# Seven partial products in layer one's second and third pair, and the x sums of that layer made in its first pair

## The chip, the core and the metric

One core of a Trainium2 chip runs the whole program: the attention, then two feed-forward layers. Its engines are TensorE (PE; its weight loads are listed as PEld), VectorE (DVE), ScalarE (ACT), GpSimd (POOL) and SyncE (SP), which issues the transfers. Each engine takes its own instructions in order; between engines, semaphores hold an instruction until what it needs is there. The metric is the device time of one execution in microseconds (us).

## What is computed

```python
def _attn_ref(q, k, v, centroids):          # clustered attention, 2 x 8 heads, 768 x 64
    ...
    return np.matmul(attn, v)

def _moe_ref(x, w_in, w_out):               # layer one; x is 1536 x 512, d_ff 2048
    h = x @ w_in
    g = np.maximum(0.01 * h, h)
    return g @ w_out

def _moe2_ref(x, w_in, w_out):              # layer two, the same sizes
    h = x @ w_in
    r = np.maximum(h, 0.0)
    return (r * r) @ w_out
```

## The kernel before

Every float32 operand of a matmul is split into a high and a low part (`xh`, `xl` for x; `wh`, `wl` for a weight block; `gh`, `gl` for an activation), and each product of two operands is three matmuls: high by high, low by high, high by low.

The attention fills `xh` and `xl` one pair of heads at a time. For the last pair, `xsplit` writes both parts on POOL (L275 the high part, L627 the low part, from the tile `xt`).

A feed-forward layer works through d_ff in eight pairs of blocks of 128 (f = 0, 2, .., 14), and x stands in three blocks of 512 rows. A step of the first kind ("plain") is `g1` (L950: one block of h from 4 x 3 matmuls of 128x512), `acts` (L960: ACT makes `gh` at L976 and the activated h at L977, DVE the low part `gl` at L982) and `g2` (L993: four output tiles of 3 matmuls each). In the first pair the results of `g2` are copied to `acc` by ACT (L1027), in later pairs added by DVE (L1030). `acc`, `th` and `tl` lie in memory that the attention has used, so the first writes to them wait for the last readers of it.

For row blocks 0 and 1 a pair can be worked out with seven products of half the inner size in place of eight (`seven`, L1054). On the way into the layer these are P1 to P7, each 2 x 3 matmuls; they need sums of weight blocks (`sum_pieces`, L246: four POOL instructions at L267, then the split, ACT L186 and POOL L187) and sums of x, called t1 to t4, made once for each of two inner blocks kk = 0 and 1 by `t_ops` (L1267). For these, DVE first adds high and low part back together (`whole`: w12, w11, w22, w21, at L1277), POOL forms t1 to t4 (L1283), ACT writes the high parts (`th`, L1286), POOL the low parts (`tl`, L1289). t4 is written over one of the x blocks, last of all (`t_last`: ACT L1326, DVE L1327). Between the products ACT and DVE carry intermediate results (`keep` L1075: k1, k6, k5; `add` L1063: aV, aX, aW); aX reads the tile that P4 then goes on adding to, so P4 waits for it. On the way out of a pair there are M1 to M7 (L1170), with one more block of weight sums.

Before, layer one runs as follows: pairs f = 0 and f = 2 are plain throughout; f = 4 is plain on the way in (steps g00, g01, g10, g11) and has seven products on the way out; from f = 6 on there are seven on both ways. Block 2 of the rows is always plain. The x sums are spread over the steps of f = 0 and 2 by the table `SUMS`; the weight blocks arrive and are taken apart by the table `TURN` (a pair of numbers is a block and a piece of its work: 0 the load, 1 ACT's and POOL's first pass, 2 DVE's join at L225, 3 ACT's high part, 4 POOL's low part). The landing buffer `wraw` is single: a block's transfer starts when the join of the block before has ended.

The order of instructions on PE, DVE, ACT and POOL is that of the program text from f = 2 on (`manual_schedule`). In pair f = 0 a scheduler places them.

Of the kernel before, what the change touches and what calls it, by code (L numbers as in the profile page):

```python
# [99 lines left out]
def attention_moe_moe_kernel(  # L100
# [1230 lines left out]
    def step_list(m, f, prev):  # L1331
# [68 lines left out]

    def sums(m, turn):
        for op in SUMS[m].get(turn, "").split():
            name, kk = op.split(".")
            t_by[m][int(kk)][name]()

    prev = []
    for m in range(2):
        turn = 0
        for f in range(0, NF, 2):
            if (m, f) == (0, 2):  # L1410
                order.enter_context(
                    tc.manual_schedule(
                        engines={
                            mybir.EngineType.PE,
                            mybir.EngineType.DVE,
                            mybir.EngineType.Activation,
                            mybir.EngineType.Pool,
                        }
                    )
                )  # L1420
# [7 lines left out]
            for i, step in enumerate(seq):  # L1428
                step()
# [11 lines left out]
                if (m, f + 2) == SEVEN[0] and i == 8:  # L1441
                    piece((*after, 3), 0)
                sums(m, turn)
                turn += 1

# [46 lines left out]
```

## Time and profile before

| | us |
|---|---|
| median of 3 runs | 737.61 (737.54 to 737.67) |
| profiled execution, its own time | 737.28 |
| span from the first to the last instruction of it | 735.6 |
| around the span | 1.7 |
| PE busy | 729.3 (99%) |
| POOL busy | 580.0 (79%) |
| DVE busy | 555.2 (75%) |
| ACT busy | 491.3 (67%) |

The attention runs to about 250 us of the span, layer one from 231 (the two overlap) to about 480, layer two to the end. Starts of instructions are counted from the span's start. A matmul's shown length is longer than the distance to the next one, since matmuls are pipelined; distances are read from starts. A DVE, ACT or POOL instruction that is listed as running may in part be held up inside; its length then exceeds that of its kind elsewhere.

### The profile page before, as it was taken

To read this page: it belongs to the slowest core of one execution; us is meant where nothing else is said; L and a number is where in the kernel's file an instruction comes from. 1 tells how busy PE (TensorE), PEld (TensorE's weight loads), DVE (VectorE), ACT (ScalarE), POOL (GpSimd) and SP (SyncE) were. 2 spreads that over 40 slices of the span, in tenths; PEclk is the share of its full clock that TensorE was granted. 3 is DMA by queue.
4 is the path that set the end of the run, shared out by engine and by line. 5 is a ranking of instruction groups with operands and counts; after the bars stand their busy time and mean duration, and the time that the engine had idled before them with its cause. 6 is when DMAs were issued, how large, how long until landed. Compare 5 with 4: busy or idle time off the path is not lost.

```text
span 735.6 us, 11900 instructions
## 1 busy us (share of the span) xinstructions
PE 729.3 (99%) x4264; PEld 647.3 (88%) x4264; DVE 555.2 (75%) x879; ACT 491.3 (67%) x909; POOL 580.0 (79%) x534
## 2 busy tenths in 40 slices
PE   9999999999999999999999999999999999999998
PEld 8999999999998888888888888888888898888987
DVE  7999999999998535476766867787676685866847
ACT  7988988988998464456364473657748457484561
POOL 7999999999957648766787877899798786777841
PEclk9999999999999999999999999999999999999999
DMA  5694574572602311111131121211113112121004
GB/s 150 168 224 111 108 186 111 113 180 68 160 22 95 121 70 60 57 58 57 59 115 57 58 91 54 85 57 58 58 58 115 57 58 61 60 110 57 1 1 172
DMA packets 17755, 65.57 MB, mean 89 GB/s; under 512 B 3120, under 2 KB 6320, under 8 KB 12704
## 3 DMA queue, kind: packets, MB, share of 16 engines
q1 hardware_dynamic: 17696, 64.81, 30.0%
q8 instruction: 34, 0.56, 0.3%
q14 instruction: 25, 0.20, 0.1%
HBM read 43.02 MB, written 3.15 MB: 63 GB/s over the span
## 4 chain that ended last, share of the span: by engine, by line
PE 94%; ACT 2%; DVE 2%; POOL 1%; issue 1%; POOLq 0%; ACTq 0%; DVEq 0%
PE h L933 33%; PE o L1170 17%; PE h L1170 10%; PE A L597 8%; PE S L500 8%; PE T L562 7%; PE o L1011 7%; PE S L370 1%; ACT e L532 1%; DVE nm L522 1%; PE warm L310 1%; DVE el L579 1%; ACT eh L573 0%; PE dots L370 0%; POOL e L549 0%
## 5 line engine op out<-in xcount | busy, mean ns | idle before, releaser
L933 PE MATMUL h<-xl,wh 128*128 128x512 f32 x288 | 112.3, 390 | 0.0
L933 PE MATMUL h<-xh,wl 128*128 128x512 f32 x288 | 112.2, 390 | 0.0
L933 PE MATMUL h<-xh,wh 128*128 128x512 f32 x288 | 112.2, 391 | 0.0
L1124 POOL TENSOR_TENSOR gl<-t,gh 128x512 fp32r<-128x512 f32 x52 | 73.1, 1426 | 36.4 <-ACT gh L1121 26.5
L579 DVE TENSOR_TENSOR el<-T,eh 128x512 fp32r<-128x512 f32 x144 | 94.6, 683 | 2.9 <-ACT eh L573 2.2
L549 POOL TENSOR_SCALAR e<-e,r 128x768 f32<-128x768 f32 x96 | 86.3, 908 | 12.7 <-PE T L562 6.8
L532 ACT ACTIVATE e<-S,nm 128x768 f32<-128x768 f32 x96 | 87.3, 909 | 9.8 <-DVE ds L398 5.3
L522 DVE TENSOR_REDUCE nm<-S 128x1 f32<-128x768 f32 x96 | 90.9, 948 | 3.6 <-PE S L370 1.9
L187 POOL TENSOR_TENSOR wl<-ws,wh 128x1024 fp32r<-128x1024 f32 x25 | 60.5, 2419 | 41.8 <-ACT wh L186 41.8
L500 PE MATMUL S<-hb 128*128 128x384 f32 (+1 forms) x384 | 89.5, 347 | 0.1
L187 POOL TENSOR_TENSOR wl<-wt,wh 128x1024 fp32r<-128x1024 f32 x31 | 76.0, 2451 | 12.9 <-ACT wh L186 12.2
L573 ACT CAST eh<-T 128x512 fp32r<-128x512 f32 x144 | 79.7, 590 | 8.8 <-PE T L562 8.6
L597 PE MATMUL A<-eh,vv 128*128 128x256 f32 x288 | 80.3, 308 | 0.6 <-DVE xt L619 0.6
L562 PE MATMUL T<-ident,e 128*128 128x128 f32 x576 | 79.7, 273 | 0.5 <-POOL e L549 0.5
L597 PE MATMUL A<-el,vv 128*128 128x256 f32 x288 | 73.0, 283 | 0.2 <-DVE el L579 0.2
L562 PEld LDWEIGHTS T<-ident,e 128*128 128x128 f32 x576 | 68.9, 143 | 3.6 <-POOL e L549 0.7
L212 ACT ACTIVATE wt<-wraw 128x1024 f32<-128x1024 f32 (+1 forms) x33 | 36.7, 1111 | 49.6 <-POOL ws L267 46.3
L1063 DVE TENSOR_TENSOR h<-h,q 128x512 f32<-128x512 f32 x36 | 25.2, 699 | 54.2 <-PE h L933 48.6
L933 PEld LDWEIGHTS h<-xh,wh 128*128 128x128 f32 x288 | 54.1, 188 | 12.0 <-DVE gl L1124 0.9
L933 PEld LDWEIGHTS h<-xh,wl 128*128 128x128 f32 x288 | 54.0, 188 | 11.3
L500 PEld LDWEIGHTS S<-hb 128*128 128x128 f32 (+1 forms) x384 | 62.2, 189 | 1.6 <-ACT e L532 1.4
L933 PEld LDWEIGHTS h<-xl,wh 128*128 128x128 f32 x288 | 54.1, 188 | 10.6
(190 smaller groups left out, 2051.0 us busy)
## 6 DMA issues: line engine op xcount, KB each, us to landing
wraw<-w SPq DMA_DIRECT2D x32, 1024.0 KB, 4.7
hb<-spl SPq DMA_DIRECT2D x14, 576.0 KB, 4.7
hb<-spl SPq DMA_DIRECT2D x42, 192.0 KB, 5.1
rqk<-qk SPq DMA_DIRECT2D x16, 384.0 KB, 3.7
rv<-v SPq DMA_DIRECT2D x8, 384.0 KB, 3.3
out<-q SPq DMA_DIRECT2D x11, 256.0 KB, 2.2
hb<-st SPq DMA_DIRECT2D x56, 24.0 KB, 1.9
hb<-hb SPq DMA_DIRECT2D x5, 144.0 KB, 8.1
```

Of the source, the lines that this page charges most:

```text
L187: return lambda eng=nc.gpsimd: eng.tensor_tensor(out=wl, in0=t, in1=wh.bitcast(F32), op=ALU.subtract)
L500: nc.tensor.matmul(out=s[:, c, 0:HALF], lhsT=hb[0:k, a, i * 128 : (i + 1) * 128], rhs=hb[0:k, b, c * HALF : (c + 1) * HALF], start=(a == 0 ...
L522: nc.vector.tensor_reduce(out=n, in_=s_t[t][:, :, 0:HALF], axis=AX.XY, op=ALU.max, negate=True)
L532: nc.scalar.activation(out=e.rearrange("p (a b) -> p a b", a=2), in_=s_t.pop(t)[:, :, 0:HALF], func=AF.Exp, bias=n_t.pop(t), scale=1.0, ac ...
L549: nc.gpsimd.tensor_scalar(out=e_t[t], in0=e_t[t], scalar1=r_t[t // 2][:, t % 2 : t % 2 + 1], scalar2=1.0, op0=ALU.mult, op1=ALU.mult,)
L562: nc.tensor.transpose(T[:, o : o + 128], e_t[2 * u + b][:, kc * 128 : (kc + 1) * 128], ident)
L573: nc.scalar.copy(out=eh[:, 2 * g : 2 * g + 2, :].rearrange("p a b -> p (a b)"), in_=T_t[u, g])
L579: nc.vector.tensor_tensor(out=el[:, 2 * g : 2 * g + 2, :].rearrange("p a b -> p (a b)"), in0=T_t.pop((u, g)), in1=eh[:, 2 * g : 2 * g + 2, ...
L597: nc.tensor.matmul(out=A, lhsT=w, rhs=m[:, kc, :], start=(kc == 0 and i == 0), stop=(kc == KC - 1 and i == 1),)
L933: nc.tensor.matmul(out=out, lhsT=l, rhs=r, start=(first and i == 0), stop=(i == n - 1), skip_group_check=not first,)
L1124: eng.tensor_tensor(out=lo[n], in0=full[n], in1=hi[n].bitcast(F32), op=ALU.subtract)
L1170: nc.tensor.matmul(out=out, lhsT=l, rhs=r, start=(fresh and i == 0), stop=(stop and i == 2), skip_group_check=True,)
```

## The change

Pair f = 2 of layer one gets seven products on both ways, pair f = 4 on the way in as well. The table `SEVEN_TOP` orders f = 2; f = 4 uses the table that f = 6 and later use. The x sums of both inner blocks are all made in pair f = 0; of the second inner block t1, t2 and t3, and of both blocks the low parts of t1 and t2, are made by DVE. The program's order is kept from step 7 of f = 0 on, not from f = 2 on. Block 2's hidden tiles lie in other PSUM banks.

```diff
-SEVEN_PLAIN = (
...
+SEVEN_TOP = (
+    "c3.0 P1 k1 P2 aV B11h B11f bh0 P6 k6 P5 k5 B11l c3.1 c3.2 h4.0 h4.1 n0.1 bh1 P7 aX B22h B22f P3 aW n0.2 "
...
-    PLAIN = (3, 1)
+    PLAIN = (1, 1)
...
-    SEVEN = tuple((0, f) for f in range(4, NF, 2)) + tuple((1, f) for f in range(2, NF, 2))
+    SEVEN = tuple((0, f) for f in range(2, NF, 2)) + tuple((1, f) for f in range(2, NF, 2))
...
-        for name, n, b, block in (
-            ("g00", "V", 0, f0), ("g01", "U", 0, f1), ("g10", "W", 1, f0), ("g11", "X", 1, f1)
-        ):
...
-            st[f"u{j}"] = bank(1 + j * m)
+            st[f"u{j}"] = bank(1 + j * (m or f == 2))
...
-            (0, 4): SEVEN_PLAIN, (0, NF - 2): SEVEN_LAST, (1, 2): SEVEN_SEAM, (1, NF - 2): SEVEN_END
+            (0, 2): SEVEN_TOP, (0, NF - 2): SEVEN_LAST, (1, 2): SEVEN_SEAM, (1, NF - 2): SEVEN_END
...
-        def minus(out, x, y, *tag):
+        def minus(out, x, y, *tag, eng=nc.gpsimd):
             st[out] = tmp(*tag)
-            nc.gpsimd.tensor_tensor(out=st[out], in0=st[x], in1=st[y], op=ALU.subtract)
+            eng.tensor_tensor(out=st[out], in0=st[x], in1=st[y], op=ALU.subtract)
...
+            "t1D": lambda: minus("t1", "b12", "b11", eng=nc.vector),
+            "t2D": lambda: minus("t2", "b22", "t1", eng=nc.vector),
+            "t3D": lambda: minus("t3", "b22", "b12", eng=nc.vector),
+            "l1D": lambda: low(0, "t1", nc.vector),
+            "l2D": lambda: low(1, "t2", nc.vector),
...
-            7: "w12.0 w11.0", 8: "t1.0 w22.0", 9: "t2.0", 10: "h1.0",
...
+            3: "w12.0 w11.0 t1.0", 4: "w22.0 t2.0 t3.0 w21.0", 5: "t4.0 w12.1",
+            7: "h1.0 h2.0 l1D.0 l2D.0 n2.0 w11.1 t1D.1 w22.1 t2D.1 h3.0 h1.1 l0.0",
+            8: "l3.0 t3D.1 w21.1 h2.1 n2.1 t4.1 n2.2 l1D.1 l2D.1", 9: "h3.1 l3.1",
...
-            if (m, f) == (0, 2):
-                order.enter_context(
...
+                if (m, i) == (0, 7):
+                    order.enter_context(
```

What this makes of the order of instructions stands at three places. The numbers behind the names tell tiles apart; line numbers of the changed program are two higher in the attention and four lower in `t_ops`.

POOL in the first pair, from its first pass over the weight block `wraw_3849` to the low part of x of the last heads (`xl`, from `xt_3518`). Before:

```order
L219 TENSOR_SCALAR wraw_3849<-wraw_3849 128x1024
L1283 TENSOR_TENSOR q_3971<-q_3949,q_3951 128x512
L275 TENSOR_SCALAR xh_66<-xt_3518 128x768
L1283 TENSOR_TENSOR q_3991<-q_3973,q_3971 128x512
L627 TENSOR_TENSOR xl_67<-xt_3518,xh_66 128x768
```

Now:

```order
L221 TENSOR_SCALAR wraw_3849<-wraw_3849 128x1024
L1279 TENSOR_TENSOR q_3874<-q_3870,q_3872 128x512
L277 TENSOR_SCALAR xh_66<-xt_3518 128x768
L1279 TENSOR_TENSOR q_3900<-q_3898,q_3874 128x512
L1279 TENSOR_TENSOR q_3902<-q_3898,q_3870 128x512
L269 TENSOR_TENSOR ws_3971<-wt_3895 128x256
L629 TENSOR_TENSOR xl_67<-xt_3518,xh_66 128x768
L189 TENSOR_TENSOR wl_3946<-wt_3895,wh_3945 128x1024
L1279 TENSOR_TENSOR t4_3923<-q_3904,q_3900 128x512
```

One more x sum (t3 of kk = 0) and the first of the four weight sums stand ahead of the low part of x; t4 of kk = 0 stands behind the weight block that follows it.

DVE in the first pair, from the join of the same weight block (`wt_3889`, now `wt_3895`) to the low part `gl_3845` of the first activated tile of row block 1. Before:

```order
L225 SCALAR_TENSOR_TENSOR wt_3889<-wt_3889,wraw_3849 128x1024
L982 TENSOR_TENSOR gl_3845<-h_3831,gh_3844 128x512
L982 TENSOR_TENSOR gl_3884<-h_3870,gh_3883 128x512
L982 TENSOR_TENSOR gl_3923<-h_3909,gh_3922 128x512
L982 TENSOR_TENSOR gl_3967<-h_3953,gh_3966 128x512
```

Now:

```order
L227 SCALAR_TENSOR_TENSOR wt_3895<-wt_3895,wraw_3849 128x1024
L1273 TENSOR_TENSOR q_3904<-xh_66,xl_67 128x512
L1273 TENSOR_TENSOR q_3925<-xh_66,xl_67 128x512
L1285 TENSOR_TENSOR tl_3777<-q_3874,th_3776 128x512
L1285 TENSOR_TENSOR tl_3777<-q_3900,th_3776 128x512
L1273 TENSOR_TENSOR q_3976<-xh_66,xl_67 128x512
L1279 TENSOR_TENSOR q_3978<-q_3925,q_3976 128x512
L984 TENSOR_TENSOR gl_3845<-h_3831,gh_3844 128x512
L1273 TENSOR_TENSOR q_3980<-xh_66,xl_67 128x512
L984 TENSOR_TENSOR gl_3890<-h_3876,gh_3889 128x512
```

Six instructions of the x sums stand between the join and `gl_3845` where none stood. The two that write `tl` wait for ACT's `th`. On ACT, too, three casts to `th` (q_3874, q_3900, q_3902) now stand between the four copies to `acc` and the activation `gh_3844`, which before followed the copies at once.

PE at the end of the first pair's row block 0, from the first matmul that reads the last heads' high part of x for `h_3831`. Before:

```order
L933 MATMUL h_3831<-xh_66,wh_3589 128x512
L933 MATMUL h_3870<-xh_66,wh_3803 128x512
L933 MATMUL h_3909<-xh_66,wh_3589 128x512
L933 MATMUL h_3953<-xh_66,wh_3803 128x512
L933 MATMUL h_3831<-xl_67,wh_3589 128x512
```

Now:

```order
L935 MATMUL h_3831<-xh_66,wh_3589 128x512
L935 MATMUL h_3876<-xh_66,wh_3803 128x512
L935 MATMUL h_3927<-xh_66,wh_3589 128x512
L935 MATMUL h_3831<-xl_67,wh_3589 128x512
L935 MATMUL h_3831<-xh_66,wl_3590 128x512
L935 MATMUL h_3876<-xl_67,wh_3803 128x512
L935 MATMUL h_3876<-xh_66,wl_3804 128x512
L935 MATMUL h_3927<-xl_67,wh_3589 128x512
L935 MATMUL h_3927<-xh_66,wl_3590 128x512
L1013 MATMUL o_3951<-gh_3844,wh_3589 128x512
L1013 MATMUL o_3951<-gl_3845,wh_3589 128x512
L1013 MATMUL o_3951<-gh_3844,wl_3590 128x512
```

The fourth hidden tile's twelve matmuls (`h_3953`, now `h_3988`) no longer stand in front of the reads of `xl` and `gl_3845` but behind the first half of the outputs `o_3951` to `o_3963`. Counted in the order, the first matmul that reads `xl` stood 32 matmuls ahead of the first matmul of pair f = 2 and now stands 42 ahead; the first that reads `gl_3845` stood 20 ahead and now stands 35 ahead. The number of instructions on PE in front of pair f = 2 is the same in both programs.

## Rows read from the trace of the kernel before

**Rows 1.** The page: busy us (share) and instructions by engine.

```profile
PE 729.3 (99%) x4264; PEld 647.3 (88%) x4264; DVE 555.2 (75%) x879; ACT 491.3 (67%) x909; POOL 580.0 (79%) x534
```

**Rows 2.** Waits of PE: waiter <- releaser: us in total, times, longest us.

```profile
PE warm L310 <- POOL ident masks.py:199: 1.4, 1, 1.4
PE A L597 <- DVE xt L619: 0.6, 1, 0.6
```

**Rows 3.** Timeline of PE: start us, length us, instruction, [idle before <- releaser].

```profile
258.18 0.39 PE L933 MATMUL h<-xl,wh 128*128 128x512 f32 x1
...
265.51 0.39 PE L933 MATMUL h<-xh,wh 128*128 128x512 f32 x1
...
334.87 0.39 PE L933 MATMUL h<-xh,wh 128*128 128x512 f32 x1
```

**Rows 4.** Timeline of POOL, up to the low part of the last heads' x.

```profile
248.03 1.12 POOL L219 TENSOR_SCALAR wraw<-wraw 128x1024 int32<-128x1024 uint32 x1 [1.28 <-DMA wraw<-w]
250.44 1.29 POOL L1283 TENSOR_TENSOR q<-q 128x512 f32<-128x512 f32 x1 [1.29 <-DVE q L1277]
251.70 1.27 POOL L275 TENSOR_SCALAR xh<-xt 128x768 fp32r<-128x768 f32 x1
252.95 2.25 POOL L1283 TENSOR_TENSOR q<-q 128x512 f32<-128x512 f32 x1
255.16 1.84 POOL L627 TENSOR_TENSOR xl<-xt,xh 128x768 fp32r<-128x768 f32 x1
```

**Rows 5.** Timeline of DVE, around x sums, a join and a `gl`.

```profile
249.61 0.68 DVE L1277 TENSOR_TENSOR q<-xh,xl 128x512 f32<-128x512 f32 x1
...
250.82 1.46 DVE L1277 TENSOR_TENSOR q<-xh,xl 128x512 f32<-128x512 f32 x1
252.21 1.84 DVE L225 SCALAR_TENSOR_TENSOR wt<-wt,wraw 128x1024 int32<-128x1024 int32 x1
...
270.66 1.23 DVE L225 SCALAR_TENSOR_TENSOR wt<-wt,wraw 128x1024 int32<-128x1024 int32 x1 [0.42 <-ACT wt L212]
271.81 1.77 DVE L1277 TENSOR_TENSOR q<-xh,xl 128x512 f32<-128x512 f32 x1
...
285.93 0.69 DVE L982 TENSOR_TENSOR gl<-h,gh 128x512 fp32r<-128x512 f32 x1 [0.33 <-ACT h L977]
```

**Rows 6.** Timeline of POOL, beside and after those, and a 128x768 scaling alone.

```profile
229.44 0.90 POOL L549 TENSOR_SCALAR e<-e,r 128x768 f32<-128x768 f32 x1
...
256.96 2.40 POOL L187 TENSOR_TENSOR wl<-wt,wh 128x1024 fp32r<-128x1024 f32 x1
...
271.16 1.87 POOL L1289 TENSOR_TENSOR tl<-q,th 128x512 fp32r<-128x512 f32 x1 [10.61 <-ACT th L1286]
...
285.68 1.30 POOL L1283 TENSOR_TENSOR q<-q 128x512 f32<-128x512 f32 x1 [1.23 <-DVE q L1277]
...
291.00 0.75 POOL L267 TENSOR_TENSOR ws<-wt 128x256 f32<-128x256 f32 x1
```

**Rows 7.** Timeline of ACT: the first copies to `acc`, an activation, a weight split.

```profile
254.08 1.05 ACT L186 CAST wh<-wt 128x1024 fp32r<-128x1024 f32 x1 [2.58 <-DVE wt L225]
257.04 2.06 ACT L1027 COPY acc<-o 128x512 f32<-128x512 f32 x4 [1.90 <-POOL xl L627]
258.95 0.64 ACT L976 ACTIVATE gh<-h 128x512 fp32r<-128x512 f32 x1
...
268.43 0.60 ACT L976 ACTIVATE gh<-h 128x512 fp32r<-128x512 f32 x1 [2.02 <-PE h L933]
```

**Rows 8.** Timeline of PE at the very start: its first matmuls, then six more.

```profile
1.41 4.21 PE L310 MATMUL warm<-ident 128*128 128x128 f32 x18 [1.41 <-POOL ident masks.py:199]
...
5.62 1.05 PE L310 MATMUL warm<-ident 128*128 128x128 f32 x6
```

**Rows 9.** Windows of the whole core: each engine's busy us (instructions), clock, DMA.

```profile
360.00:400.00 40.00, 40.00 (x178) 33.01 (x177) 27.95 (x42) 19.35 (x29) 31.02 (x25) 1.00 0.20 69
```

**Rows 10.** The page's transfers: out <- in, queue, kind xcount, KB each, us to landing.

```profile
wraw<-w SPq DMA_DIRECT2D x32, 1024.0 KB, 4.7
```

More of the change, by code (lines that the diff above doesn't have):

```diff
@@ L77 @@
 )
-SEVEN_PLAIN = (
-    "n0.1 g00 B11h B11f c3.1 c3.2 bh0 n0.2 B11l n1.0 g01 B21h B21f B21l bh1 n0.3 n0.4 g10 B12f T1 n1.1 "
-    "n1.2 g11 B22h B22f T3 T2 T1h T2h T1l T4 u0 T2l u0h u0f u0l T3h T3l n1.3 n1.4 "
-) + SEVEN_REST + " h4.0 h4.1"
+SEVEN_TOP = (
[4 rows of a table added]
+)
 SEVEN_TWO = SEVEN_FIRST.replace("B11h B11f P5 k5", "B11h P5 k5 B11f").replace(
@@ L1089, in seven @@
             )
-        for name, n, b, block in (
-            ("g00", "V", 0, f0), ("g01", "U", 0, f1), ("g10", "W", 1, f0), ("g11", "X", 1, f1)
-        ):
-            ops[name] = lambda n=n, b=b, block=block: prod(
-                n, [w_in(block, k) for k in ks], [x_in(k, b) for k in ks], True
-            )
         for name, n in (("k1", "U"), ("k6", "U"), ("k5", "W")):
@@ L1279, in whole, with low @@
             )
-        def minus(out, x, y, *tag):
+        def minus(out, x, y, *tag, eng=nc.gpsimd):
             st[out] = tmp(*tag)
-            nc.gpsimd.tensor_tensor(out=st[out], in0=st[x], in1=st[y], op=ALU.subtract)
+            eng.tensor_tensor(out=st[out], in0=st[x], in1=st[y], op=ALU.subtract)
         def high(i, t):
             nc.scalar.copy(out=th[:, i, kk], in_=st[t])
-        def low(i, t):
-            nc.gpsimd.tensor_tensor(
+        def low(i, t, eng=nc.gpsimd):
+            eng.tensor_tensor(
                 out=tl[:, i, kk], in0=st[t], in1=th[:, i, kk].bitcast(F32), op=ALU.subtract
@@ L1365, in attention_moe_moe_kernel @@
     TURN = (
-        ((0, 1),), ((0, 2),), ((1, 0),), ((0, 3),), ((0, 4), (1, 1)),
-        ((1, 2),), ((2, 0),), ((1, 3), (1, 4), (3, 0)), ((2, 1),), ((2, 2),),
+        ((0, 1),), ((0, 2),), ((1, 0),), ((0, 3),), ((0, 4), (1, 1)), ((1, 2),), ((1, 3), (1, 4)),
     )
@@ L1399, in attention_moe_moe_kernel, with sums @@
     t_by = [[t_ops(m, kk) for kk in range(2)] for m in range(2)]
-    def sums(m, turn):
+    def sums(m, turn, after, later):
         for op in SUMS[m].get(turn, "").split():
             name, kk = op.split(".")
-            t_by[m][int(kk)][name]()
+            if name in t_by[m][0]:
+                t_by[m][int(kk)][name]()
+            else:
+                piece((*(after if name[0] == "n" else later), int(name[1])), int(kk))
     prev = []
     for m in range(2):
-        turn = 0
         for f in range(0, NF, 2):
-            if (m, f) == (0, 2):
-                order.enter_context(
[L1412 to L1420, printed above, removed]
             after = pair_after(m, f)
@@ L1428, in attention_moe_moe_kernel @@
             for i, step in enumerate(seq):
+                if (m, i) == (0, 7):
+                    order.enter_context(
+                        tc.manual_schedule(
+                            engines={
+                                mybir.EngineType.PE,
+                                mybir.EngineType.DVE,
+                                mybir.EngineType.Activation,
+                                mybir.EngineType.Pool,
+                            }
+                        )
+                    )
                 step()
@@ L1440, in attention_moe_moe_kernel @@
                     piece((*later, k - 3) if k > 2 else (*after, k), j, *eng)
[L1441 to L1444, printed above, removed]
+                sums(m, i, after, later)
 _OUT = (1536, 512)
```

6 rows, old and new, of tables (SEVEN_TOP, SUMS) are left out of this document.

## The prediction

> **What bounds the kernel now.** I read the page's busy line first, then PE's waits, then the engines' timelines at the two places that the change reorders. PE is busy for 729.3 of 735.6 us [rows 1], which alone proves little, since matmuls overlap. The waits settle it: after the start, PE's longest wait is 0.6 us [rows 2]. The pace is even as well: from the first matmul of pair f = 2 at 265.51 to that of f = 6 at 334.87 [rows 3] there are 306 matmuls in the order, all of 512 columns: 69.36 / 306 = 0.2267 us each. So a matmul less is worth 0.2267 us, as long as PE goes on finding its operands; and any wait put into PE's queue goes to the end undiminished, because no later stretch has idle time that could take it up.
>
> **What the change removes.** Seven products in place of eight save 6 matmuls on the way into a pair (42 for 48) and 6 on the way out. f = 2 saves 12, f = 4 saves 6: 18 x 0.2267 = 4.08 us off PE.
>
> **What it adds, and where that is hidden.** Three more blocks of weight sums (four POOL instructions, an ACT split, a POOL split each), six more k copies on ACT and as many sums on DVE, 22 instructions more on DVE in all. Spread over the two pairs of some 30 us each they have room: in 360 to 400, where seven products run on both ways, POOL is busy 31.02 of 40, DVE 27.95, ACT 19.35, and PE never waits [rows 9]. I take nothing for them there, apart from one place named below. The first pair is another matter, because there the x sums are put in front of what PE reads next.
>
> **First wait: the low part of the last heads' x.** Had PE no wait, pair f = 2 would begin at 265.51 as before, since equally many instructions precede it. The first reader of this `xl` now stands 42 matmuls ahead of that, so PE wants it at 265.51 - 42 x 0.2267 = 255.99; before it was 258.18 [rows 3]. When does POOL have it? Its row begins with the pass over the weight block at 248.03, which waited for a transfer [rows 4]; that transfer starts after the same join as before, so this stays. Then come t1, the high part, t2, t3, a weight sum, and `xl`.
>
> How long these take depends on DVE, which now does x sums and a join at the same time. The rows show what happens then. An x sum on DVE takes 0.68 alone, but 1.46 and 1.77 when POOL is at work; the join takes 1.23 or 1.84 [rows 5]. POOL's subtraction takes 1.29 alone, but 2.25 at 252.95, beside the join, and 1.87 at 271.16 [rows 4, 6]. The ends fit turns, not sharing: POOL's subtraction at 271.16 ends at 273.03, DVE's sum listed from 271.81 ends 0.55 later, at 273.58; POOL's at 252.95 ends 1.15 after the join's end at 254.05. A `gl`, which reads one of its operands from PSUM, takes 0.69 beside POOL at 285.93 [rows 5, 6]. So I let DVE instructions with both operands in SBUF and POOL instructions take turns, at their lengths alone. The Trainium skill (SBUF — State Buffer, section SBUF: two separate sides) says so in general: the port pair that the two engines share is locked for a whole instruction and the loser is blocked. Taken instead as two engines side by side, the same work gives the lower bound below; the rows are with the rule.
>
> In turns, from the pass's end at 249.15: DVE w22 0.68, POOL t1 1.29, DVE join 1.23, POOL high part 0.90, DVE w21 0.68, POOL t2 1.29, t3 1.29 (DVE's next sum waits for it), weight sum 0.75, DVE w12 0.68, POOL `xl` 1.84 [rows 4 to 6]: 10.63, less some 0.3 for starts that overlap the end before: 259.5. Side by side the DVE terms (3.27) fall out: 256.4. PE waits 3.5 us, at least 0.4.
>
> **Second wait, behind it: `gl_3845`.** Its reader stands 35 matmuls ahead of f = 2: wanted at 257.58. ACT's copies to `acc` wait for the end of `xl` (they did at 257.04) and the next instruction begins 1.91 later [rows 7]. That is now the first cast to `th`, not the activation: with 0.6 it ends at 262.05. DVE's next instruction, the low part of t1, waits for it, and behind it are queued the low part of t2, w11, t1 of kk = 1, and only then `gl_3845`. POOL meanwhile does a split of 2.40 and t4 of 1.29, to 263.15. In turns then: DVE 0.68, weight sum 0.75, DVE 0.68, weight sum 0.75, DVE 0.68, weight sum 0.75, DVE 0.68 = 4.97, then `gl` 0.69, less 0.4 of overlap: 268.4 [rows 5, 6]. PE resumes 268.4 - 257.58 = 10.8 us late, the first wait included. Side by side it is 256.4 + 0.04 + 1.91 + 0.6 + 4 x 0.62 + 0.69 = 262.1, that is 4.5 late; with every turn lost to a longer POOL instruction it is near 12. I take 10.8, since the rows show turns each time the two meet.
>
> **Third wait, in f = 2: P4.** Counting from the end of the first pair's last hidden tile: an activation begins 0.2 after such an end (the twelve matmuls from 265.51 end at 265.51 + 12 x 0.2267 = 268.23, their tile's activation begins at 268.43) [rows 3, 7]; ACT and DVE give its low part at 2.0; DVE t3 and w21 end at 3.3; POOL's t4 of kk = 1 waits for w21 and ends at 5.1, the weight split at 8.1, a low part at 9.4, four weight sums at 12.3; ACT's split (1.05) and first cast of t4 at 14.0. DVE's low part of t4 then meets POOL's next split (2.40, to 15.9), the second meets POOL's next pass (1.12), so they end at 16.5 and 18.2; aX (0.69) is queued behind them: 18.9. P4 waits for aX and is due 72 matmuls after the end counted from, at 16.3. That is 2.6 us; side by side aX ends at 15.9 and it is 0.
>
> After P4 I find POOL's splits ahead of their readers by 2 us or more, up to f = 4 and in it.
>
> **Sum.** In the profiled execution: 737.28 - 4.08 + 10.8 + 2.6 = 746.6. The median of the runs is 0.3 above that execution: 746.9.
>
> **Rivals.**
> - *PE's clock falls in the wait.* In this case PE stands nearly still from 256.0 to 268.4, far longer than anywhere in this trace [rows 2], and the granted clock reads 1.00, as in 360 to 400 [rows 9], so no row shows a fall. But the first 18 matmuls, after a PE that had done nothing, took 4.21 us, 0.234 each; the next six took 1.05 together, 0.175 each with the last one's tail [rows 8]. If PE comes back at 1.2 GHz for a stretch like that, half of 4.2 us is lost: 749.0. The Trainium skill (TensorE: Matmul & The Clock Gate, section HAM oscillation — how this bites in real kernels) says that a long idle gap puts PE back to the lower clock. By that rule the 749.0 would be the result. Chance 0.20.
> - *The turns cost about half.* The two engines meet less often than my walk has it, for instance because a cast comes before a split begins: 741 to 744. Chance 0.15.
> - *No turns at all.* The lower bounds hold: -4.08 + 4.5 + 0 = +0.4, 738.0, no change that can be told. Against it are the 1.77 and 2.25. Chance 0.09.
> - *Faster: the waits are covered.* The one thing ahead of everything is the weight block's transfer, 4.7 us [rows 10] and late until 248.03. If it landed 2 us sooner and the engines ran side by side, `gl_3845` would be there at 260.1, 2.5 late, and 4.08 - 2.5 = 1.6 us would be won: 736.0. From 261.7 on, 4.08 after 257.58, nothing is won. Against it: its start waits for the same join as before. Chance 0.06.
> - That the matmuls are not removed is excluded by the order of instructions.
>
> **How the numbers follow.** My forecast, both waits in turns, has 0.50: 746.9, give or take 1.3. The range runs from 740.5 to 750.0; it takes in the forecast, the clock's case and the half-cost case, and leaves out the last two rivals and the tails, together 0.2. A measurement of this kernel can tell about 0.2% (1.5 us) from no change. Faster by more: 0.06. Within: 0.09. Slower: 0.85.
>
> **What would show it.** PE's waits in the new trace should name POOL's `xl` (some 3.5 us) and DVE's `gl` at about 268 (some 7 us), both ahead of f = 2, and DVE's h or POOL's and ACT's t4 ahead of P4 (2.6). `xl` should end near 259.5; x sums on DVE should be 1.3 us and more beside POOL. f = 2 should begin at about 276.3, not 265.5. I am wrong if `xl` ends by 257, if DVE's x sums stay at 0.7 beside POOL, or if ACT's copies to `acc` no longer wait for `xl`. The granted clock behind the wait tells the first rival apart.

## The result, and the profile after

The changed kernel takes 747.82 us (median of five runs, 747.26 to 751.12), the kernel before in the same comparison 737.61: a ratio of 1.015, with an interval of 1.0127 to 1.0172. The profiled execution took 747.66 us, 10.4 more than that of before.

PE does 18 matmuls less and is busy 0.4 us longer than in [rows 1]:

```profile
PE 729.7 (98%) x4246; PEld 646.2 (87%) x4246; DVE 572.4 (77%) x901; ACT 498.4 (67%) x921; POOL 595.3 (80%) x546
```

PE's waits (as [rows 2]: waiter <- releaser: us in total, times, longest). Four are new, and they are the three places that the prediction names:

```profile
PE o L1013 <- DVE gl L984: 3.6, 1, 3.6
PE h L935 <- POOL xl L629: 2.6, 1, 2.6
PE h L935 <- DVE h L1065: 1.9, 1, 1.9
...
PE o L1013 <- ACT gh L978: 1.2, 1, 1.2
```

Where they stand in PE's timeline (start us, length us, instruction, [idle before <- releaser]):

```profile
258.59 0.80 PE L935 MATMUL h<-xl,wh 128*128 128x512 f32 x1 [2.56 <-POOL xl L629]
...
262.71 0.50 PE L1013 MATMUL o<-gh,wh 128*128 128x512 f32 x1 [1.20 <-ACT gh L978]
266.82 0.80 PE L1013 MATMUL o<-gl,wh 128*128 128x512 f32 x1 [3.61 <-DVE gl L984]
267.42 0.63 PE L1013 MATMUL o<-gh,wl 128*128 128x512 f32 x1
267.84 0.63 PE L1013 MATMUL o<-gh,wh 128*128 128x512 f32 x1
...
272.07 0.40 PE L935 MATMUL h<-xl,wh 128*128 128x512 f32 x1
...
277.29 0.39 PE L935 MATMUL h<-xh,wh 128*128 128x512 f32 x1
...
344.78 0.39 PE L935 MATMUL h<-xh,wh 128*128 128x512 f32 x1
```

The row at 266.82 is the first reader of `gl_3845`, the one at 277.29 the first matmul of f = 2 (265.51 in [rows 3]), the one at 344.78 that of f = 6 (334.87). Behind 266.82 the matmuls start 0.43 apart, not 0.2267: PE runs at half rate up to 272. The windows say so too (each engine's busy us and instructions; the number behind POOL's is the granted clock, 1.00 being 2.4 GHz and 0.50 being 1.2 GHz):

```profile
258.00:260.00 2.00, 1.41 (x3) 1.16 (x4) 0.00 (x0) 1.44 (x4) 2.00 (x2) 0.59 0.00 0
...
268.00:270.00 2.00, 2.00 (x7) 1.54 (x6) 1.52 (x3) 0.00 (x0) 0.00 (x0) 0.50 0.00 0
```

So f = 2 begins 11.78 us late: 266.82 - 257.58 = 9.24 by the waits, and 277.29 - 266.82 - 35 x 0.2267 = 2.54 by the clock. P4 loses 2.03 more. With the 4.08 saved that makes 9.7. The start of f = 6 is 9.91 us later than before, the last matmul 9.65 (741.59, before 731.94), the end of the span 10.2: some 0.5 us more is lost behind the last matmul, which I did not follow.

What PE waited for. POOL from the first x sum to `xl` (compare [rows 4]):

```profile
249.32 1.60 POOL L1279 TENSOR_TENSOR q<-q 128x512 f32<-128x512 f32 x1
250.89 1.80 POOL L277 TENSOR_SCALAR xh<-xt 128x768 fp32r<-128x768 f32 x1
252.67 2.96 POOL L1279 TENSOR_TENSOR q<-q 128x512 f32<-128x512 f32 x2
...
256.29 2.24 POOL L629 TENSOR_TENSOR xl<-xt,xh 128x768 fp32r<-128x768 f32 x1
```

ACT's copies to `acc` and its first casts to `th` (compare [rows 7]), then DVE from the low part of t1 to `gl_3845`:

```profile
258.56 2.06 ACT L1029 COPY acc<-o 128x512 f32<-128x512 f32 x4 [5.48 <-POOL xl L629]
260.48 1.69 ACT L1282 CAST th<-q 128x512 fp32r<-128x512 f32 x3
```

```profile
261.16 2.63 DVE L1285 TENSOR_TENSOR tl<-q,th 128x512 fp32r<-128x512 f32 x2 [4.29 <-ACT th L1282]
263.71 1.21 DVE L1273 TENSOR_TENSOR q<-xh,xl 128x512 f32<-128x512 f32 x1
264.95 1.09 DVE L1279 TENSOR_TENSOR q<-q 128x512 f32<-128x512 f32 x1
266.08 0.69 DVE L984 TENSOR_TENSOR gl<-h,gh 128x512 fp32r<-128x512 f32 x1
...
288.12 4.04 DVE L1328 TENSOR_TENSOR xl<-t,xh 128x512 fp32r<-128x512 f32 x2 [7.10 <-ACT xh L1327]
292.09 1.28 DVE L1065 TENSOR_TENSOR h<-h,q 128x512 f32<-128x512 f32 x2
```

Four instructions that take 0.68 each alone take 4.92 here, beside POOL, and the `gl`, which reads one operand from PSUM, takes 0.69. The last two rows are the third wait: the two low parts of t4, 4.04 us, and `aX` behind them.

### The profile page after: what moved, and what is told of

Read it like the earlier page. It is cut to its first block, busy times and chain, and to the rows that moved or that the text cites. A ratio compares the mean times of both kernels' runs of the same rounds, so it can differ in the third digit from the quotient of the medians.

```text
span 745.8 us, 11914 instructions
## 1 busy us (share of the span) xinstructions
PE 729.7 (98%) x4246; PEld 646.2 (87%) x4246; DVE 572.4 (77%) x901; ACT 498.4 (67%) x921; POOL 595.3 (80%) x546
## 4 chain that ended last, share of the span: by engine, by line
PE 82%; POOL 6%; DVE 4%; ACT 3%; issue 2%; DMA 2%; POOLq 0%; DVEq 0%; ACTq 0%
PE h L935 28%; PE o L1166 17%; PE h L1166 10%; PE A L599 7%; PE S L502 7%; PE T L564 7%; PE o L1013 3%; DMA wraw<-w 2%; PE S L372 1%; ACT e L534 1%; POOL ws L269 1%; POOL wl L189 1%; DVE nm L524 1%; POOL gl L1120 1%; PE warm L312 1%
## 5 line engine op out<-in xcount | busy, mean ns | idle before, releaser
L935 PE MATMUL h<-xl,wh 128*128 128x512 f32 x272 | 106.9, 393 | 2.6 <-POOL xl L629 2.6
L935 PE MATMUL h<-xh,wh 128*128 128x512 f32 x272 | 106.3, 392 | 1.9 <-DVE h L1065 1.9
L935 PE MATMUL h<-xh,wl 128*128 128x512 f32 x272 | 106.7, 393 | 0.0
L1120 POOL TENSOR_TENSOR gl<-t,gh 128x512 fp32r<-128x512 f32 x56 | 80.0, 1450 | 31.9 <-ACT gh L1117 21.8
L189 POOL TENSOR_TENSOR wl<-ws,wh 128x1024 fp32r<-128x1024 f32 x28 | 68.4, 2441 | 40.5 <-ACT wh L188 40.5
L1065 DVE TENSOR_TENSOR h<-h,q 128x512 f32<-128x512 f32 x42 | 29.2, 698 | 59.6 <-PE h L935 54.1
L935 PEld LDWEIGHTS h<-xl,wh 128*128 128x128 f32 x272 | 51.6, 190 | 13.1 <-POOL xl L629 3.0
L935 PEld LDWEIGHTS h<-xh,wh 128*128 128x128 f32 x272 | 51.2, 188 | 13.5 <-issue 2.3
L1120 DVE TENSOR_TENSOR gl<-h,gh 128x512 fp32r<-128x512 f32 x70 | 47.8, 685 | 18.5 <-ACT h L1102 7.8
```

The costliest lines, as they stand in the source:

```text
L189: return lambda eng=nc.gpsimd: eng.tensor_tensor(out=wl, in0=t, in1=wh.bitcast(F32), op=ALU.subtract)
L935: nc.tensor.matmul(out=out, lhsT=l, rhs=r, start=(first and i == 0), stop=(i == n - 1), skip_group_check=not first,)
L1120: eng.tensor_tensor(out=lo[n], in0=full[n], in1=hi[n].bitcast(F32), op=ALU.subtract)
```

## The experiments

The theory under test: PE waits for what is queued ahead of its operands, DVE and POOL slow each other down in turns, and the clock is a cost by itself. The rivals: the added x sums cost as much wherever they stand (the load theory); DVE is slow by itself; the clock falls for another reason than PE's idle time. The median of before is named with each group of runs.

**Undoing the order on ACT and DVE** (before: 737.83 for this and the next three).

```diff
+                if (m, f, i) == (0, 0, 7):
+                    gh, gl = parts[0, 2, 0]
+                    nc.scalar.copy(out=th[:, 0, 0, 0:1], in_=gh[:, 0:1].bitcast(F32))
+                    nc.vector.tensor_copy(out=tl[:, 0, 0, 0:1], in_=gl[:, 0:1].bitcast(F32))
                 sums(m, i, after, later)
```

> The changed kernel with one thing undone: in the queues of ScalarE and VectorE the three activations and low parts of the first pair (gl_3845 first) stand ahead of the first three th casts, of the two tl low parts and of w11, t1 of kk = 1. A copy of one column on each engine holds these back; xl and its place on GpSimd are untouched. Queue theory (PE waits for what is queued ahead of gl_3845): the wait for xl stays 2.6 us; the activation begins at about 260.5, right behind the copies to acc, gl_3845 is ready at 262.3 in place of 266.8, so its reader starts some 4.4 us sooner; how many half-rate matmuls are left is open, so 742 to 744 in place of 747.8. Load theory (the added x sums cost PE as much wherever they stand, because DVE and POOL slow each other down): another wait of the same size appears a few us later, 746 to 748. If the delayed x sums are now late for P5 and P6 of f = 2, a wait before f = 2's seventh matmul group shows it.

Measured: 743.11 us, ratio 1.0089 (1.0059 to 1.0120). The profiled execution is the slowest of the five (749.02): in the attention PE waited 2.1 us at 18 us, with half rate behind it (granted clock 0.83 from 20 to 40 us), so that everything from before 250 us on is 5.1 us later. The row below thus answers to 262.4, as the queue theory had it:

```profile
267.54 0.50 PE L1013 MATMUL o<-gl,wh 128*128 128x512 f32 x1 [0.71 <-DVE gl L984]
```

The order on the two queues, with the half-rate matmuls that it brought, is 4.7 of the 10 us. No wait of the size of that for `gl_3845` came up later; that of P4 stayed (2.5 in place of 1.9, with some 1.6 us of half rate behind it).

**Keeping PE busy in the wait.**

```diff
+                if (m, f, i) == (0, 0, 7):
+                    d = bank(0)
+                    wd = weights[0, 0, 0][0]
+                    for _ in range(12):
+                        nc.tensor.matmul(
+                            out=d, lhsT=wd[:, 0:128], rhs=xl[:, HP - 1, N : 2 * N], start=True, stop=True
+                        )
                 step()
```

> The changed kernel with twelve extra 512-column matmuls on PE, between the readers of the last heads' xl and the reader of gl_3845; their product is used by nothing. They read xl, so they cannot run before it. Nothing else moves. Clock theory (the granted clock stays low because PE stands still from 261.3 to 266.8, and this alone makes the matmuls behind the wait half as fast): the waits for xl (2.6 us) and gl_3845 (its reader at 266.8) stay, but the 35 matmuls from there to f = 2 take 35 x 0.2267 = 7.9 us in place of 10.5; f = 2 begins at about 274.8 in place of 277.3, and the time is 745.3. If the clock falls for another reason than the idle time, or takes as long to rise as before from 266.8 on, f = 2 stays at 277.3 and the time at 747.8; if the twelve matmuls themselves end later than gl_3845 is ready, it is over 748.

Measured: 746.14, ratio 1.0112 (1.0095 to 1.0129): 1.7 below the changed kernel, not 2.5. PE's timeline of this run:

```profile
259.86 2.89 PE L1434 MATMUL h<-xl,wh 128*128 128x512 f32 x12
...
266.64 0.50 PE L1013 MATMUL o<-gl,wh 128*128 128x512 f32 x1 [3.64 <-DVE gl L984]
...
267.91 0.63 PE L1013 MATMUL o<-gh,wh 128*128 128x512 f32 x1
268.33 0.63 PE L1013 MATMUL o<-gl,wh 128*128 128x512 f32 x1
...
271.55 0.39 PE L935 MATMUL h<-xh,wh 128*128 128x512 f32 x1
```

The twelve ran at full rate, were done early, and left 3.6 us of idle time. The clock fell after that, 1.3 us after PE was at work again, and was back by 271.55. So the idle time was too little covered for a verdict, and e6 was made.

**Taking POOL away from beside DVE.**

```diff
-            7: "h1.0 h2.0 l1D.0 l2D.0 n2.0 w11.1 t1D.1 w22.1 t2D.1 h3.0 h1.1 l0.0",
-            8: "l3.0 t3D.1 w21.1 h2.1 n2.1 t4.1 n2.2 l1D.1 l2D.1", 9: "h3.1 l3.1",
+            7: "h1.0 h2.0 l1D.0 l2D.0 w11.1 t1D.1 w22.1 t2D.1 h3.0 h1.1 l0.0",
+            8: "t3D.1 w21.1 h2.1 t4.1 l3.0 n2.0 n2.1 n2.2 l1D.1 l2D.1", 9: "h3.1 l3.1",
```

> The changed kernel with GpSimd's weight sum out of the place ahead of xl, and its other three weight sums and the low part of t3 out of the stretch in which VectorE makes tl, tl, w11 and t1 (they come behind t4 of kk = 1 now). VectorE's four instructions and their order are untouched. xl should end 0.7 us sooner (257.8), and so the copies to acc and the casts. Turn theory (a VectorE instruction with both operands in SBUF and a GpSimd instruction take turns): the four VectorE instructions, 4.9 us from the start of the first to gl_3845 before, meet one GpSimd instruction (t4) in place of four and take 3.0 to 3.7 us, the last three at 0.65 to 0.7 each; gl_3845's reader starts at 263.5 to 264.8. Theory of separate engines (VectorE is as slow whatever GpSimd does): 4.9 us again, reader at 266.1. The whole time says nothing on this, since the weight sums are then late for P6 of f = 2: PE waits there some 4 us for wh or wl of that block, about 750 in all.

DVE of this run:

```profile
259.83 2.38 DVE L1285 TENSOR_TENSOR tl<-q,th 128x512 fp32r<-128x512 f32 x2 [2.08 <-ACT th L1282]
262.13 0.68 DVE L1273 TENSOR_TENSOR q<-xh,xl 128x512 f32<-128x512 f32 x1
262.85 0.69 DVE L1279 TENSOR_TENSOR q<-q 128x512 f32<-128x512 f32 x1
263.57 0.69 DVE L984 TENSOR_TENSOR gl<-h,gh 128x512 fp32r<-128x512 f32 x1
```

The same four instructions take 3.74 us in place of 4.92, and the two that meet no POOL instruction take 0.68 and 0.69. `gl_3845`'s reader starts at 264.31, as the turn theory has it; DVE is not slow by itself. The time is 755.12 (one run): the weight sums are late for f = 2. PE waits 5.6 us there, not for the sums themselves, as expected, but for copies to `acc` that stand on ACT behind the cast of these sums, and half rate follows.

**`xl` first on POOL.**

```diff
             st[out] = tmp(*tag)
+            if (m, kk, out) == (0, 0, "t2"):
+                nc.gpsimd.tensor_copy(out=st[out][:, 0:1], in_=xl[:, HP - 1, S : S + 1].bitcast(F32))
...
-            7: "h1.0 h2.0 l1D.0 l2D.0 n2.0 w11.1 t1D.1 w22.1 t2D.1 h3.0 h1.1 l0.0",
-            8: "l3.0 t3D.1 w21.1 h2.1 n2.1 t4.1 n2.2 l1D.1 l2D.1", 9: "h3.1 l3.1",
+            7: "h1.0 h2.0 l1D.0 l2D.0 w11.1 t1D.1 w22.1 t2D.1 h3.0 h1.1 l0.0",
+            8: "l3.0 t3D.1 w21.1 h2.1 n2.0 n2.1 t4.1 n2.2 l1D.1 l2D.1", 9: "h3.1 l3.1",
```

> The changed kernel with GpSimd's order turned: the low part of the last heads' x (xl) comes right behind t1 and the high part, and t2, t3 and the weight sum that stood ahead of it come behind it. A copy of one column out of xl into t2's tile holds them back. Because t2 and t3 are ready later, the second and third th cast and one of the two tl low parts fall behind the activations by themselves. Queue theory: xl ends at 254.9 in place of 258.5, so PE does not wait for it; the copies to acc follow at once, gl_3845 is ready at about 259.3, PE waits some 1.7 us for it and its clock stays at 1.00, f = 2 begins at about 267.3 in place of 277.3, and the time is 738 (736 to 741 with a new wait of up to 3 us in f = 2 for x sums that are late). Load theory: the time stays at 746 to 748.

Measured: 742.33, ratio 1.0064 (1.0049 to 1.0079), between the two forecasts. The wait for `xl` is gone, but the reader of `gl_3845` starts at 261.79, not 259.3, after waits of 0.8 and 3.1 us, and the clock falls again. What I had not seen is a DVE instruction ahead of `gl_3845`, the x sum w12 of kk = 1, whose buffer POOL's t2 had to free first:

```profile
259.28 1.74 DVE L1273 TENSOR_TENSOR q<-xh,xl 128x512 f32<-128x512 f32 x1 [1.30 <-POOL q L1281]
261.04 1.88 DVE L984 TENSOR_TENSOR gl<-h,gh 128x512 fp32r<-128x512 f32 x3
```

**The third wait alone** (before: 737.47 for this and the next two).

```diff
-    "... B11l c3.1 c3.2 h4.0 h4.1 n0.1 bh1 P7 aX ..."
+    "... B11l h4.0 h4.1 c3.1 c3.2 n0.1 bh1 P7 aX ..."
```

> The changed kernel with two entries of f = 2's order exchanged: the casts and low parts of t4 (h4.0 h4.1) ahead of the two steps c3.1 c3.2 of the fourth weight block, so that ScalarE casts t4 before it waits for that block's sums. Nothing ahead of f = 2 changes. Queue theory of the third wait (aX is queued on VectorE behind the two low parts of t4, which come late because their casts stand behind a cast that waits for GpSimd's weight sums): PE's wait of 1.9 us ahead of P4 goes, the low parts start about 3 us sooner, and the time is 747.8 - 1.9 = 745.9, less if the clock no longer falls there in some executions. If aX is late for another reason (P7, k5), the wait stays and the time is 747.8. If the cast of the fourth block is now late, a new wait shows at M6 or M5.

Measured: 747.13, ratio 1.0133 (1.0118 to 1.0148). P4's wait is gone from the trace, no other came for it. The time fell by 0.7 only, and the intervals of the two kernels overlap, so that this alone shows no gain. In the profiled execution the row that waits for `xl` is 0.56 later than in the changed kernel, and half rate behind `gl_3845` costs 2.9 in place of 2.5. So the trace shows the cause of the third wait, but the time does not show its 2 us; that a wait of this kind goes into the time is shown in f = 4, by e9 and e11 below.

**Covering the wait with 24 matmuls** (the edit of e2 with `range(24)`).

> As e2_fill, with 24 extra matmuls in place of 12, so that PE is at work from the readers of xl to within 1.3 us of gl_3845. Clock theory: with so short an idle time the granted clock stays at 1.00 behind it, f = 2 begins 35 x 0.2267 = 7.9 us after the reader of gl_3845, which is where it was, and the time is 745.0 to 745.5, about 2.5 below the changed kernel and 0.9 below e2_fill, of which the rest of the 10 us stays, since both waits for xl and gl_3845 stay. If the idle time is not what brings the clock down, matmuls at 0.43 apart show again behind the wait and the time is 746 or more.

Measured: 745.68, ratio 1.0109 (1.0094 to 1.0124). In the profiled execution PE was at half rate behind the wait for `xl`, and with work at hand the clock was back before `gl_3845`:

```profile
258.44 0.79 PE L935 MATMUL h<-xl,wh 128*128 128x512 f32 x1 [2.41 <-POOL xl L629]
...
267.08 0.39 PE L1013 MATMUL o<-gl,wh 128*128 128x512 f32 x1
...
275.02 0.39 PE L935 MATMUL h<-xh,wh 128*128 128x512 f32 x1
```

From the reader of `gl_3845` to f = 2 it is 7.94 us, 35 x 0.2267, at full rate throughout. Some 2.1 us of the loss are the clock's, and with the second stretch of idle time filled it did not fall there.

**All three repairs together.** As e1, e4 and e5, with these sums:

```diff
+            3: "w12.0 w11.0 t1.0", 4: "w22.0 t2.0 t3.0 w21.0", 5: "t4.0",
+            7: "h1.0 h2.0 l1D.0 l2D.0 w12.1 w11.1 t1D.1 w22.1 t2D.1 h3.0 h1.1 l0.0",
+            8: "l3.0 h2.1 n2.0 n2.1 n2.2 l1D.1 l2D.1 t3D.1 w21.1 t4.1", 9: "h3.1 l3.1",
```

> The changed kernel with all its matmuls saved, and with e1, e4 and e5 together: xl ahead of t2, t3 and the weight sums on GpSimd; the x sum w12 of kk = 1, which in e4 stood ahead of gl_3845 on VectorE and waited for t2, behind it; the three activations and low parts ahead of all casts of x sums; t4's casts ahead of the fourth block's; and, since the x sums are later now, wl of the third block ahead of t4 of kk = 1 on GpSimd. Queue theory: xl is no wait, gl_3845 is ready at 259.3, PE waits 1.5 to 2 us in all, without a fall of the clock, f = 2 begins at 267.3, the wait ahead of P4 is gone, and the time is 737.8 - 4.1 + 1.8 = 735.5 (735 to 737 with a wait of up to 1.5 us ahead of P6 for the low part of t2). Load theory: at least half of the loss of the changed kernel stays, 741 or more.

Measured: 738.34, ratio 1.0012 (1.0002 to 1.0021). Nine tenths of the loss are gone, so the load theory falls in the form I gave it. But the 735.5 of the queue theory failed too, and the 4.1 us do not show: f = 2 begins at 266.65, and PE loses time in it at two new waits, 1.3 us for a copy to `acc` behind a cast that waits for t2, and 0.8 at P6.

**The same with a better order** (before: 737.63).

```diff
-    "c3.0 P1 k1 P2 aV B11h B11f bh0 P6 k6 P5 k5 B11l c3.1 c3.2 h4.0 h4.1 ..."
+    "c3.0 P1 k1 P2 aV B11h B11f bh0 th3.1 tl3.1 P6 k6 P5 k5 B11l h4.0 h4.1 c3.1 c3.2 ..."
...
-            if (m, kk, out) == (0, 0, "t2"):
+            if (m, kk, out) == (0, 0, "t1"):
...
+            3: "w12.0 w11.0 t1.0", 4: "w22.0 t2.0 t3.0 w21.0",
+            7: "h1.0 h2.0 l1D.0 l2D.0 t4.0 n2.0 w12.1 w11.1 h3.0 t1D.1 n2.1 h1.1 w22.1 t2D.1 l0.0",
+            8: "l3.0 n2.2 l1D.1", 9: "h2.1 l2D.1 t3D.1 w21.1 t4.1",
```

> As e7_all_three, with what was still late there moved: on GpSimd xl stands ahead of t1 too, and the weight sums of the third block ahead of the low part of t3; on ScalarE the cast of the third weight block stands ahead of, and the second cast of t2 behind, the first pair's last copies to acc (in e7 these copies stood behind a cast that waited for t2, and the reader of o waited 1.1 us for them); the cast of t3 of kk = 1 stands behind k1 (in e7 P6 waited 0.6 us for k1 there). Same work, same matmuls. Queue theory: PE waits 0 to 0.8 us ahead of f = 2, which begins at 265.5 to 266.4, no wait over 0.6 us in f = 2, and the full 4.1 us of the saved matmuls shows but for that: 737.5 - 4.1 + 0.5 = 733.9 (733.4 to 735). If a part of the loss came from the added work itself and not from its place, the time stays at 736 or more. If the low part of t2 is late now, a wait ahead of P6 of up to 1.5 us shows, 735.5.

Measured: 739.04, ratio 1.0014 (0.9996 to 1.0031); the forecast of 733.9 failed. PE's waits, and one window of this run, then the same window of before:

```profile
PE o L1013 <- DVE gl L984: 1.3, 1, 1.3
PE h L935 <- ACT q L1077: 1.0, 2, 0.7
PE o L1166 <- DVE gl L1120: 0.6, 1, 0.6
...
PE h L935 <- POOL tl L1289: 0.5, 1, 0.5
```

```profile
257.00:275.00 18.00, 15.91 (x69) 12.60 (x69) 17.19 (x18) 9.94 (x20) 14.21 (x11) 1.00 0.01 1
```

```profile
257.00:275.00 18.00, 18.00 (x80) 14.77 (x80) 6.39 (x8) 12.40 (x24) 7.31 (x6) 1.00 0.17 61
```

DVE (third pair of numbers) is taken up for 17.2 of 18 us, against 6.4 before, and POOL for 14.2, the time that each is held up by the other included. My reading is that another order would only choose who comes late; e12 below tries it.

**One part of the change alone** (before: 737.69 for this and the next).

```diff
-    PLAIN = (3, 1)
+    PLAIN = (2, 1)
...
-            st[f"u{j}"] = bank(1 + j * m)
+            st[f"u{j}"] = bank(1 + j * (m or f == 4))
...
-            (0, 4): SEVEN_PLAIN,
+            (0, 4): SEVEN_TOP,
...
-                if (m, f + 2) == SEVEN[0] and i == 8:
-                    piece((*after, 3), 0)
```

> The kernel before with one part of the change alone: pair f = 4 has seven products on the way in too (6 matmuls less), f = 2 stays plain on both ways, and the x sums stay where they were, spread over the steps of f = 0 and f = 2. Matmul theory (a matmul less is worth 0.2267 us where PE never waits, and the loss of the changed kernel comes from x sums pressed into f = 0): no wait over 0.6 us appears, and the time falls by 1.36 us, 737.5 to 736.2. Load theory (the k copies, weight sums and splits that go with the seven products cost PE about as much as they save): 737.5 or more, with a wait in f = 4.

Measured: 742.63, ratio 1.0056 (1.0037 to 1.0075): slower, by one wait. It is the third wait, in f = 4 this time:

```profile
316.08 0.47 PE L935 MATMUL h<-xh,wh 128*128 128x512 f32 x1 [3.80 <-DVE h L1065]
```

```profile
308.96 3.97 DVE L1329 TENSOR_TENSOR xl<-t,xh 128x512 fp32r<-128x512 f32 x2 [6.77 <-ACT xh L1328]
312.86 2.47 DVE L1032 TENSOR_TENSOR acc<-o,acc 128x512 f32<-128x512 f32 x4
315.25 1.28 DVE L1065 TENSOR_TENSOR h<-h,q 128x512 f32<-128x512 f32 x2
```

-1.36 + 3.96 + 1.6 (eight matmuls at half rate) = 4.2 of the 4.9 measured.

**Twelve of the 18 matmuls, with more time for the x sums.** `SEVEN` from f = 2 on, `PLAIN` as above, f = 2 by `SEVEN_PLAIN` with the x sums written in between, f = 4 by the table of f = 6.

```diff
+    "n0.1 g00 B11h B11f c3.1 c3.2 bh0 n0.2 xh1.0 B11l n1.0 xl1.0 xh2.0 xt3.0 g01 xw21.0 B21h B21f B21l bh1 n0.3 "
+    "n0.4 g10 xl2.0 xh3.0 B12f T1 n1.1 xt4.0 n1.2 g11 B22h B22f T3 xl3.0 T2 T1h T2h T1l xw12.1 xw11.1 T4 u0 T2l "
...
```

> The kernel before with two parts of the change: seven products on the way out of f = 2 and on the way into f = 4 (12 of the 18 matmuls), the way into f = 2 stays plain, and the x sums begin in f = 0 as before and go on between the products of f = 2, where they are wanted only in f = 4. Matmul theory: 2.72 us less, 734.8, as long as the x sums fit between f = 2's other work; they have some 36 us there, against some 20 in the changed kernel. Turn theory with too much work in f = 2 (GpSimd and VectorE in turns): a wait of 1 to 3 us in f = 2 or at P6 of f = 4, 736 to 738.

Measured: 746.33, ratio 1.0113 (1.0084 to 1.0142). Both theories were too low. PE waits 2.1 us for a `gl` behind two x sums on DVE (2.4 us in turns) and 3.1 us for an addition to `acc` whose chain hangs on an activation cast behind a weight cast that waits for POOL, each with half rate behind it. It speaks for the queue mechanism, not on whether a better order would win.

**The one part, mended** (before: 737.34 for this and the next). As e9, with

```diff
-    "... bh0 P6 k6 P5 k5 B11l c3.1 c3.2 h4.0 h4.1 n0.1 bh1 P7 aX B22h ..."
+    "... bh0 h4.0 h4.1 P6 k6 P5 k5 B11l c3.1 c3.2 n0.1 P7 aX bh1 B22h ..."
```

> As e9_f4_alone, whose only wait was that ahead of P4 of f = 4 (3.8 us: aX behind the two low parts of t4, 4.0 us in turns with GpSimd, and behind four additions to acc). Moved: the casts and low parts of t4 ahead of P6, where VectorE and GpSimd have time, and P7 and aX ahead of the last hidden tile of the pair before (bh1), so that twelve matmuls lie between aX and P4. Matmul theory: no wait over 0.6 us, and 6 x 0.2267 = 1.36 us less than before: 736.3 (736.0 to 736.8). If a wait for aX or for the x sums stays, 737.5 or more.

Measured: 736.53, ratio 0.9988 (0.9979 to 0.9997): faster than both kernels. No wait over 0.6 us is left. The low parts of t4 now fall into a stretch in which DVE has time, and `aX` is no longer behind them:

```profile
303.67 2.37 DVE L1329 TENSOR_TENSOR xl<-t,xh 128x512 fp32r<-128x512 f32 x2 [1.66 <-ACT xh L1328]
308.11 0.70 DVE L1065 TENSOR_TENSOR h<-h,q 128x512 f32<-128x512 f32 x1 [2.08 <-ACT q L1077]
```

The gain is 0.8 of the 1.36 us; 1.36 lies within the interval. In the profiled execution the last matmul starts 1.42 us sooner than before (730.52, 731.94), and 0.5 of that is lost behind it.

**Half of the x sums left out.** As e8, without the x sums of kk = 1: P5, P6 and P7 read those of kk = 0 twice and P4 the plain x, so the kernel does not compute the layer; it serves the timing alone.

```diff
+            7: "h1.0 h2.0 l1D.0 l2D.0 t4.0 n2.0 h3.0 n2.1 l0.0",
+            8: "l3.0 n2.2",
```

> As e8_order, but without the x sums of the second inner block: t1 to t4 of kk = 1, their casts and low parts and the four sums behind them are left out (P5, P6 and P7 of layer one read those of kk = 0 twice, P4 the plain x). All matmuls, weight sums, k copies and activations stay. Turn theory (what e8 still loses is that VectorE's and GpSimd's x sums, one at a time, do not fit between the end of the attention and f = 2): the wait for gl_3845 stays (1.3 us, it lies ahead of those sums), the waits for k1, tl and gl in f = 2 go (2.4 us in all in e8): 739.0 - 2.5 = 736.5 (735.8 to 737). If the rest of the loss is due to the other added work (k copies, weight sums, splits), the waits in f = 2 stay and the time is 738.5 or more.

Measured: 735.41, ratio 0.9973 (0.9963 to 0.9983). All the waits of e8 in f = 2 are gone, and one is left, ahead of it:

```profile
PE o L1013 <- DVE gl L984: 1.1, 1, 1.1
```

The first matmuls of f = 2 and f = 6:

```profile
267.15 0.39 PE L935 MATMUL h<-xh,wh 128*128 128x512 f32 x1
...
332.47 0.39 PE L935 MATMUL h<-xh,wh 128*128 128x512 f32 x1
```

From f = 2 to f = 6 it is 65.32 us, 288 x 0.2267 with nothing lost; in e8 it is 68.70 (266.80 to 335.50). All other added work (the k copies, weight sums and splits) is in this run, and PE never waits for it there. So the 3.4 us that e8 lost between f = 2 and f = 6 come with the second half of the x sums; even the forecast of 736.5 was too high. Still, only 1.9 of the 4.08 us are won: f = 2 begins 1.6 us later than before, and some 1.1 us go behind the last matmul (729.24, before 731.94), where the last sum waits 0.5 us for a transfer of the output. Neither was followed.

## Why the prediction was right, step by step

The forecast was 746.9, the time 747.8. The mechanism of the waits and their three places were right. That the total came within 0.9 us is in part luck: the waits had been walked 2.1 us too long together, and the clock, which the sum left out, cost 2.5.

- *The matmuls saved, 4.08.* They are saved: from 277.29 to 344.78 it is 67.49 us, less 2.03 at P4 = 65.46, and 288 x 0.2267 is 65.3.
- *First wait, 3.5 forecast.* It was 2.6: `xl` ended at 258.53, not 259.5. In POOL's rows above, t1 took 0.31 more than alone, the high part 0.90, t2 and t3 together 0.38, `xl` 0.40. So DVE's three sums and its join cost POOL 2.0 us, where I had put the sums' full lengths, 3.27 less 0.3. A turn cost the other engine less than its length; I had taken an overlap off once, not at each hand-over. (The lower bound beside it, 256.4, is 256.2 by its own terms; nothing hangs on that.) The Trainium skill (SBUF — State Buffer, section SBUF: two separate sides) has the loser fully blocked. The rows agree that one engine holds up the other, but POOL's weight sums (0.75 alone, [rows 6]) and DVE's sums (0.68) in turns start every 1.14 us (POOL at 262.06, 263.20, 264.33), not every 1.43.
- *Second wait, 10.8 late in all.* It was 9.24: 1.0 by `xl`, some 0.6 by the same overlap in the turns (5.66 from the first cast's end to `gl_3845`, 6.35 forecast). e1 and e3 show that both parts of the term are real: without the four instructions ahead, PE goes on 4.4 us sooner, and without POOL beside them they take 3.74.
- *Third wait, 2.6.* The trace has 1.87 (2.03 lost). e5 removes it by its named cause, and e11 removes the same wait in f = 4.
- *The clock.* This was the term that I left out of the sum and gave to a rival at 0.20, with 2.1 us. It came, with 2.54, so what happened is that rival's case with shorter waits, not the case that I gave 0.50. Had the waits been as long as I walked them, 749.4 would have been the time. The step that failed is this: from "no row shows a fall" I took that none was likely, though no row of before shows a wait that long. The Trainium skill (TensorE: Matmul & The Clock Gate, section HAM oscillation — how this bites in real kernels) had said that it falls; the trace agrees, with a granted clock of 0.50 behind the wait of 3.6 us, and shows 0.59 behind the shorter one of 2.6 us too.
- *The side-by-side rival (738.0)* is refuted by e3: beside POOL the lengths are 1.1 to 1.3, alone 0.68. *Half the turns (741 to 744)* is out by the trace: the turns came at each place that the walk has, and the time lies outside.
- *The transfer* ended when it did before (POOL's pass began at 248.12, 248.03 in [rows 4]), so the faster rival had no ground.

What the prediction did not ask is whether another order could save the 4.08 us. e7 and e8 won back 9 of 10 us but not these, and e12 names the larger part of the reason: the x sums of kk = 1 cost 3.4 us between f = 2 and f = 6. Whether a split of the x sums between f = 0 and f = 2 could win with all 18 matmuls stays open.

## What to carry to other kernels

Before work is moved forward, add up, for the stretch it moves into, the time of DVE instructions with two SBUF operands and of POOL instructions as if they were one queue, and look at what then stands ahead of the operands that PE reads next; an engine's spare share of the whole span says nothing on that. Price a long wait of PE with the half rate behind it: in these executions most waits of 2.1 us and more brought it, some 1.2 to 2.9 us of PE's time each, and those of 1.9 and less did not. A change that saves several times over is best tried in parts: the third of it that needed no x sum sooner was worth 0.8 us, the whole cost 10.

## What the runs showed of the hardware that I had not expected

Behind waits of the same length the clock did not always do the same. Behind the 2.4 to 2.6 us for `xl` it was at 1.2 GHz at once in the changed kernel and in e6, but at 2.4 in e1 and e2. In e2 it fell 1.3 us after PE had taken up work again, in e9 1.0 us. In e8, where no wait was over 1.3 us, it stayed at 2.4. With PE at work from 266.82 on it was back by 272.07 in the changed kernel, and in e6 within the 24 matmuls. What decides the moment of the fall was not separated.

A POOL instruction on one column takes its turn like any other. The one-column copy of e4 took 0.65 us beside a low part on DVE; in e7, with DVE idle, 0.18:

```profile
257.37 0.65 POOL L1280 COPY q<-xl 128x1 f32<-128x1 f32 x1
```

```profile
257.03 0.18 POOL L1280 COPY q<-xl 128x1 f32<-128x1 f32 x1
```
